# A recurrent attention loop with streamed weights: four places instead of five, one block more kept, 16 streamed

## The chip, the cores and the metric

The kernel runs on one core of one Trainium2 chip. The metric is the time of the whole program on the device in microseconds; lower is better. An execution under the profiler gives the span from the first to the last instruction, and a trace from which every view below is read.

## The reference

Two independent computations, put side by side along the last axis. Part A is a recurrent transformer layer: 2048 tokens in 64 segments of 32, each with 8 memory rows that are the first 8 output rows of the segment before. 32 heads of 128, model width 1024.

```python
mem = mem0
for s in range(n_seg):                                   # 64 segments
    xs = x[:, s * seg_len:(s + 1) * seg_len, :]
    h = jnp.concatenate([mem, xs], axis=1)               # 8 + 32 rows
    q = jnp.einsum('btd,dhe->bhte', h, Wq)               # Wq, Wk, Wv: [1024, 32, 128]
    k = jnp.einsum('btd,dhe->bhte', h, Wk)
    v = jnp.einsum('btd,dhe->bhte', h, Wv)
    scores = jnp.einsum('bhqe,bhke->bhqk', q, k) * scale
    scores = jnp.where(mask[None, None], scores, -1000000000.0)
    p = softmax(scores, axis=-1)
    o = jnp.einsum('bhqk,bhke->bhqe', p, v)
    o = jnp.einsum('bhte,hed->btd', o, Wo)               # Wo: [32, 128, 1024]
    mem = o[:, :M, :]
    outs.append(o[:, M:, :])
```

Part B is a long convolution: a kernel `K` of 2048 steps for each of 1024 channels is made from complex exponentials, and `u` is convolved with it by Fourier transforms.

## The kernel before

The program runs part B first (`part_b`), then part A (`part_a`). While part B runs, work of part A that doesn't depend on the recurrence is done beside it: projections of the last 8 rows of each segment, kept in DRAM (`PKd`), transposed inputs (`XTd`), and loads of weight blocks that will stay in SBUF.

**Weight blocks.** The four weights are cut into 64 blocks of 128 x 2048 bf16, 512 KB each. A key names a block: `("k", t, kc)` is the part of Wk for input rows 128 kc to 128 kc + 127 and the 16 heads of half t, likewise "q" and "v"; `("o", u)` holds heads 2u and 2u+1 of Wo. In every segment all 64 are needed once. Not all fit in SBUF, so there are three kinds:

- resident blocks (`RESIDENT`, line 171): loaded once, 34 of them during part B and the rest at their first use in segment 0;
- two blocks in PSUM (`KEPT`, line 28): `("k", 0, 7)` and `("o", 15)`, copied to pieces in SBUF by VectorE in each segment (`fetch`, line 278);
- streamed blocks (`STREAM`, `STREAM_O`, lines 25 and 26): 17 of them, fetched from a DRAM copy (`WD`) in every segment. They share `SLOTS` = 5 places in SBUF, tags w0 to w4, in turn.

**Order of a segment.** Lines 435 to 526 write it out by hand (`tc.manual_schedule()`; program order is the order on each engine): projections k0, q0, k1, q1, v0, v1 with `quads` (line 321; eight units of four matmuls, one for each block), transposes, scores and softmax of the two halves between them, then the output projection `oproj` over o0 to o15 (line 423), and at the end the result `ob`, whose first 8 rows go by two transposes (`tro`, line 523) into `hT`, the transposed input of the next segment. All projections of a segment wait for that: the loop is a chain from segment to segment.

**How a streamed block is loaded.** `unit` (line 235) is called by `quads` and `oproj` for each key. For a streamed one it does this:

```python
between.pop(key, lambda: None)()
t_ = wst.tile([128, 2048], BF16, name="wst", tag="w%d" % (loads[0] % SLOTS))
loads[0] += 1
nc.sync.dma_start(out=t_[:], in_=WD[key][:])
```

The load goes on SyncE's (SP's) queue. It must wait until TensorE has released the same place, that is until the streamed block `SLOTS` earlier has been used; SP is free to run that far ahead. SP's queue is in order: a transfer that waits holds up the ones behind it.

**Side transfers.** Three kinds of smaller transfers use the same queue, and `between` says ahead of which streamed block each is put. `load_pk` (line 292) fetches the projected last rows of this segment, 192 KB; its tile `pk` is also used as working space (`lb0a`, `pb1`), so it waits for the last reader in the segment before, `pv_l` at line 510. `stores` (line 309) writes the previous segment's `ob` to `OLd` and to the output, 64 KB each; it waits for the last copy into `ob` (line 526). `load_xt` (line 297) fetches the next segment's transposed input, 48 KB; its tile shares a place (tag F) with `lb0b`, and `put_xt` copies it into `hT`.

Of the kernel before, what the change touches and what calls it, by code (L numbers as in the profile page):

```python
# [21 lines left out]

STREAM = {("k", 0): (0, 5), ("q", 0): (1, 5), ("k", 1): (0, 3), ("q", 1): (0, 4), ("v", 0): (0, 4), ("v", 1): (0, 4)}
STREAM_O = (0, 4, 8, 11, 13)

KEPT = {("k", 0, 7): (("B", 0, 512), ("C", 512, 512), ("A", 1024, 512), ("F", 1536, 256), ("L", 1792, 256)),
        ("o", 15): (("B", 0, 512), ("C", 512, 512), ("E", 1024, 512), ("F", 1536, 256), ("L", 1792, 256))}
SLOTS = 5  # L30


def weight_blocks(Wq, Wk, Wv, Wo):
# [15 lines left out]
def streamed_keys():  # L49
    return [key for key in [(m, t, kc) for (m, t), kcs in STREAM.items() for kc in kcs] + [("o", u) for u in STREAM_O]]  # L50

# [136 lines left out]
def part_a(ctx, tc, x, mem0, src, WD, HE, seg_len, out_a, ahead, W_res, rest):  # L188
# [44 lines left out]
    between = {}  # L233

    def unit(key):
# [8 lines left out]
# [3 lines that stand above are left out]
# [45 lines left out]
    def load_pk(j):  # L292
        pk = pers.tile([128, 768], BF16, name="pk", tag="pk")
        nc.sync.dma_start(out=pk[:], in_=PKd[j])
        return pk

    def load_xt(j):
        xt = work.tile([128, KC, XM], BF16, name="xt", tag="F")
        nc.sync.dma_start(out=xt[:].rearrange("p k r -> p (k r)"), in_=XTd[j])
        return xt  # L300

    def put_xt(xt):
        nc.gpsimd.tensor_copy(out=hT[:, :, 0:XM], in_=xt[:])  # L303
# [5 lines left out]
    def stores(s, ob):  # L309
        nc.sync.dma_start(out=OLd[s // 8][:, 256 * (s % 8):256 * (s % 8) + 256], in_=ob[:, 1, :])  # L310
        rows = out_a[s * SL:s * SL + SL, :].rearrange("r (q d) -> q r d", q=4)
        if s + 1 < NS:

            nc.sync.dma_start(out=rows, in_=ob[:, 0, :])
        else:
            for q in range(4):
                nc.sync.dma_start(out=rows[q][0:XM], in_=ob[32 * q:32 * q + XM, 0, :])

    fetch(("k", 0, 7))
    for s in range(NS):  # L320
        def quads(m, t, kcs, a=None):
            if a is None:

                pool, tag = {("q", 0): (ps_sc, "sc"), ("q", 1): (ps_pv, "pv")}.get((m, t), (ps_acc, "acc"))
                a = pool.tile([128, 512], F32, name="acc", tag=tag)
            for kc in kcs:
                w = unit((m, t, kc))
                for g in range(4):
                    for o_, rhs in columns(w, 512 * g, 512):
                        nc.tensor.matmul(a[32 * g:32 * g + 32, o_:o_ + rhs.shape[1]], lhsT=hT[:, kc, :], rhs=rhs,  # L330
                                         start=(kc == 0), stop=(kc == KC - 1), tile_position=(0, 32 * g), skip_group_check=True)
            return a
# [90 lines left out]
        def oproj(po, us, oT):  # L423
            for u in us:
                w = unit(("o", u))
                for hh in range(2):
                    h = 2 * u + hh
                    for qt in range(4):
                        nc.tensor.matmul(po[32 * qt:32 * qt + 32, :], lhsT=oT[:, h % 4, (h % 16) // 4, :],  # L429
                                         rhs=columns(w, 1024 * hh + 256 * qt, 256)[0][1],  # L430
                                         start=False, stop=(h == 31), tile_position=(0, 32 * qt), skip_group_check=True)
# [2 lines left out]


        pks = []
        between["q", 0, 1] = lambda: pks.append(load_pk(s))
        if s:
            between["k", 1, 3] = lambda: stores(s - 1, ob)
        a = quads("k", 0, range(KC))  # L440
        k0 = evac(a, "A")
        a = quads("q", 0, range(KC))
# [66 lines left out]
        oproj(pp[:, 1, :], (7,), o0)  # L509
        pv_l(pl_, 1, V1, L1)  # L510
        if s + 1 < NS:
            between["o", 13] = lambda: put_xt(load_xt(s + 1))
        oproj(pp[:, 1, :], range(8, 14), o1)
        fetch(("o", 15))
        oproj(pp[:, 1, :], range(14, 16), o1)
        ob = work.tile([128, 2, 256], BF16, name="ob", tag="E")
# [677 lines left out]
def kernel(  # L1194
# [55 lines left out]
    with ExitStack() as ctx_a:  # L1250
        part_a(ctx_a, tc, A_x[0], A_mem0[0], src, WD, A_Wo.shape[0] * A_Wo.shape[1], seg_len, out_a, ahead, W_res, rest)
# [35 lines left out]
```

## Time and profile before

| | us |
|---|---|
| median of 3 runs | 2549.41 |
| lowest and highest run | 2538.42, 2555.1 |
| span of the profiled execution | 2562.5 |
| first matmul of the loop | 881.5 |
| end of the last turn from a segment to the next | 2468.6 |
| TensorE busy (matmuls) | 2055.3 (80%) |
| VectorE busy | 1498.0 (58%) |
| ScalarE busy | 1023.9 (40%) |
| GpSimd busy | 311.6 (12%) |

The span is all that the page tells of the profiled execution's own time; it is 13 us over the median of the runs, which were not profiled.

How to read the views: busy rows and DMA rows come in 40 slices of the span, each digit the busy share in tenths. A line of a wait says engine and source line, what it waited for, and then the total in us, the number of times and the longest. A line of the timeline says start, duration, engine, source line, operation, and in brackets the engine's idle time before it with what ended that. For SP, "SPq" lines are the issues of transfers: they begin when the transfer's waits are over, and end when SP is free for the next one; the data move later. L330 are the projections, L429 the output projection, L247 the loads of streamed blocks (tile `wst`), L294, L299, L310 and L314 the side transfers `pk`, `xt`, `OLd` and `out`.

Besides these views the prediction uses the landing events of transfers that the trace records: the time of the last update of a transfer's semaphore.

### The profile page before, as it was taken

The numbers are of one execution on the slowest core, as the hardware profiler recorded it, in microseconds if no ns is written. First come the engines' busy times: TensorE is split into PE (matmuls) and PEld (weight loads), VectorE is DVE, ScalarE is ACT, GpSimd is POOL, SyncE is SP. The second block draws the span as 40 slices with busy tenths as digits, with TensorE's granted clock in tenths as the row PEclk, the third lists the DMA queues.
The fourth block names the chain that finished last, engine by engine and source line by source line (L and its number), as shares of the span: only waits on it lengthen the run. The fifth ranks groups of instructions, "written<-read, shape, count | busy, mean of one in ns | idle before, by whom it ended". The sixth has DMA issues, their size and how long they took to land.

```text
span 2562.5 us, 76703 instructions
## 1 busy us (share of the span) xinstructions
PE 2055.3 (80%) x32856; PEld 1101.7 (43%) x32902; DVE 1498.0 (58%) x3224; ACT 1023.9 (40%) x1550; POOL 311.6 (12%) x601
## 2 busy tenths in 40 slices
PE   1588888857697778888888888888888888888879
PEld 1355555633242334444444444444444444444444
DVE  9687777879985245545454554545455454545450
ACT  6788788961121223323333332323333232333321
POOL 2133424442001100000000000000000000000020
PEclk6799999978898889999999999999999999999999
DMA  5665756543346999999999999999999999999992
GB/s 135 174 190 155 229 173 176 149 146 116 125 132 212 339 382 379 378 380 365 386 362 381 372 386 369 362 373 369 390 383 384 380 364 374 369 370 373 374 384 74
DMA packets 382387, 763.18 MB, mean 298 GB/s; under 512 B 118678, under 2 KB 210806, under 8 KB 379998
## 3 DMA queue, kind: packets, MB, share of 16 engines
q1 hardware_dynamic: 363006, 700.44, 76.1%
q0 software_dynamic: 14128, 39.99, 4.6%
q10 hardware_dynamic: 4912, 17.84, 2.0%
q8 instruction: 257, 4.21, 0.6%
q14 instruction: 84, 0.69, 0.1%
HBM read 703.35 MB, written 67.88 MB: 301 GB/s over the span
## 4 chain that ended last, share of the span: by engine, by line
DMA 33%; PE 28%; DVE 17%; ACT 9%; issue 8%; SPq 1%; POOL 0%; ACTq 0%; DVEq 0%; POOLq 0%
DMA wst<-WD_k 16%; PE acc L330 12%; DMA wst<-WD_o 10%; PE pp L429 3%; DMA wst<-WD_v 3%; PE pe L552 2%; ACT sn L1019 2%; PE pro L151 2%; PE tr L341 2%; ACT kM L994 1%; DVE piece L269 1%; PE ups L850 1%; ACT E L991 1%; PE pro L138 1%; ACT ev L336 1%
## 5 line engine op out<-in xcount | busy, mean ns | idle before, releaser
L330 PEld LDWEIGHTS <-hT 128*32 128x32 bf16 x12352 | 326.8, 97 | 474.1 <-issue 256.0
L330 PE MATMUL acc<-wst,hT 128*32 128x512 bf16 x3072 | 313.6, 393 | 163.3 <-DMA wst<-WD_k 67.4
L336 ACT CAST ev<-acc 128x512 bf16<-128x512 f32 x384 | 225.1, 586 | 414.4 <-PE acc L330 409.4
L429 PEld LDWEIGHTS <-oT 128*32 128x32 bf16 x8192 | 204.5, 97 | 116.6 <-issue 90.4
L269 DVE TENSOR_SCALAR piece<-keep 128x256 int32<-128x256 int32 (+1 forms) x640 | 191.4, 363 | 56.5 <-PE pp L429 31.1
L429 PE MATMUL pp<-W_o,oT 128*32 128x256 bf16 x5120 | 212.5, 277 | 6.8 <-DMA W_o<-in_A_Wo_dram 6.8
L330 PE MATMUL acc<-W_v,hT 128*32 128x512 bf16 x3072 | 211.1, 379 | 0.3 <-DMA W_v<-in_A_Wv_dram 0.3
L368 DVE TENSOR_REDUCE mx<-sc 128x8 f32<-128x320 f32 x128 | 62.4, 487 | 251.8 <-PE sc L361 251.6
L330 PE MATMUL acc<-W,hT 128*32 128x512 bf16 x2560 | 205.7, 392 | 0.0
L342 DVE COPY KT<-tr 128x512 bf16<-128x512 bf16 x64 | 27.2, 425 | 264.3 <-PE tr L341 264.3
L429 PE MATMUL pp<-wst,oT 128*32 128x256 bf16 x2560 | 129.2, 278 | 39.3 <-DMA wst<-WD_o 30.3
L342 ACT COPY QT<-tr 128x512 bf16<-128x512 bf16 x128 | 75.0, 586 | 192.6 <-PE tr L341 191.7
L1159 PE MATMUL yp<-Bt,mi 128*128 128x512 bf16 x379 | 115.5, 411 | 41.5 <-DMA mi<-MId 32.2
L416 ACT CAST oT<-pv 128x512 bf16<-128x512 f32 x128 | 75.1, 586 | 169.3 <-PE pv L402 166.9
L349 POOL COPY KT<-pk 128x128 bf16<-128x128 bf16 x128 | 37.6, 293 | 816.0 <-PE sc L361 454.4
L330 PE MATMUL acc<-W_q,hT 128*32 128x512 bf16 x1792 | 135.1, 383 | 0.0
L995 DVE SCALAR_TENSOR_TENSOR nr<-kM,ptt 128x656 f32<-128x656 f32 x128 | 104.9, 833 | 44.3 <-ACT kM L994 44.1
L151 PE MATMUL pro<-xTl,wsl 128*128 128x512 bf16 x493 | 116.6, 384 | 12.7 <-DVE kst L155 7.5
L370 ACT ACTIVATE sc<-sc 128x320 f32<-128x320 f32 x128 | 54.0, 422 | 154.8 <-DVE sc L369 148.0
L330 PE MATMUL acc<-W_k,hT 128*32 128x512 bf16 x1536 | 112.6, 401 | 0.0
L303 POOL COPY hT<-xt 128x192 bf16<-128x192 bf16 x64 | 22.2, 347 | 728.1 <-DMA xt<-XTd 442.0
L1075 PE MATMUL hps<-KT,MF 128*128 128x512 bf16 x374 | 93.3, 395 | 19.9 <-DVE x L1088 19.4
(288 smaller groups left out, 3766.7 us busy)
## 6 DMA issues: line engine op xcount, KB each, us to landing
wst<-WD_o SPq DMA_DIRECT2D x320, 512.0 KB
wst<-WD_k SPq DMA_DIRECT2D x256, 512.0 KB
wst<-WD_q SPq DMA_DIRECT2D x256, 512.0 KB
wst<-WD_v SPq DMA_DIRECT2D x256, 512.0 KB
Ud<-ux POOLq DMA_DIRECT2D x16, 1024.0 KB, 4.8
uq<-Ud SPq DMA_DIRECT2D x32, 512.0 KB
pk<-PKd SPq DMA_DIRECT2D x64, 192.0 KB
wsl<-in_A_Wk_dram SPq DMA_DIRECT2D x16, 512.0 KB
```

Source lines behind the costliest of these rows:

```text
L151: nc.tensor.matmul(a[:], lhsT=w[:, kc, 128 * j:128 * j + 128], rhs=xTl[:, kc, :, :].rearrange("p s k -> p (s k)"), start=(kc == 0), stop=( ...
L269: nc.vector.tensor_scalar(out=out.bitcast(I32), in0=in_.bitcast(I32), scalar1=0, scalar2=None, op0=ALU.bitwise_or)
L330: nc.tensor.matmul(a[32 * g:32 * g + 32, o_:o_ + rhs.shape[1]], lhsT=hT[:, kc, :], rhs=rhs, start=(kc == 0), stop=(kc == KC - 1), tile_pos ...
L336: nc.scalar.copy(out=q[:], in_=a[:])
L342: eng(out=dst, in_=p[:, i, :, :, :])
L368: nc.vector.tensor_reduce(out=mx[:], in_=sc, axis=AX.X, op=ALU.max)
L370: nc.scalar.activation(out=sc, in_=sc, func=ACT.Exp, scale=scale)
L416: nc.scalar.copy(out=o[:], in_=p[:].rearrange("p a (g q) -> p a g q", g=4))
L429: nc.tensor.matmul(po[32 * qt:32 * qt + 32, :], lhsT=oT[:, h % 4, (h % 16) // 4, :], rhs=columns(w, 1024 * hh + 256 * qt, 256)[0][1], star ...
L995: v.scalar_tensor_tensor(out=nrs[e // 4][:, e % 4].rearrange("p f t j -> p f (t j)"), in0=kM[:], scalar=MAGIC, in1=ptv, op0=ALU.subtract, ...
L1075: pe.matmul(ps[:], lhsT=MF[:, 4 * rr + mc, cs, 128 * kc:128 * kc + 128], rhs=rhs, start=(i == 0 and mc == 0), stop=(i == 1 and mc == 3))
L1159: pe.matmul(yp[:], lhsT=m_[:, cs, kc, :], rhs=Bt[:, kc, half, j, c_, :], start=(n == 0), stop=(n == 15))
```

## The change

The streamed blocks have four places instead of five. The fifth place's 512 KB hold one resident block more, so 16 blocks are streamed in each segment instead of 17, and which ones they are is chosen anew: k0: 0 and 6; q0: 4; k1: 1 and 6; q1: 0 and 6; v0: 2 and 6; v1: 0 and 4; o: 0, 6, 8, 11, 14. The three side transfers are put ahead of other blocks: `pk` ahead of q0:4, `stores` ahead of k1:1, `xt` ahead of o11. They stay on SP's queue. The order of the matmuls, transposes, softmax parts and copies in a segment stays as it is; only which units read a streamed place differs.

```diff
-STREAM = {("k", 0): (0, 5), ("q", 0): (1, 5), ("k", 1): (0, 3), ("q", 1): (0, 4), ("v", 0): (0, 4), ("v", 1): (0, 4)}
-STREAM_O = (0, 4, 8, 11, 13)
+STREAM = {("k", 0): (0, 6), ("q", 0): (4,), ("k", 1): (1, 6), ("q", 1): (0, 6), ("v", 0): (2, 6), ("v", 1): (0, 4)}
+STREAM_O = (0, 6, 8, 11, 14)
...
-SLOTS = 5
+SLOTS = 4
...
-        between["q", 0, 1] = lambda: pks.append(load_pk(s))
+        between["q", 0, 4] = lambda: pks.append(load_pk(s))
         if s:
-            between["k", 1, 3] = lambda: stores(s - 1, ob)
+            between["k", 1, 1] = lambda: stores(s - 1, ob)
...
-            between["o", 13] = lambda: put_xt(load_xt(s + 1))
+            between["o", 11] = lambda: put_xt(load_xt(s + 1))
```

## The prediction

> **What bounds the kernel now.** I read the page first. Its digit rows (40 slices of 64 us) show two halves: part B up to slice 13, then the recurrent loop, where the DMA engines stand at 9 in every slice and PE at 8.
>
> ```profile
> PE   1588888857697778888888888888888888888879
> DMA  5665756543346999999999999999999999999992
> GB/s 135 174 190 155 229 173 176 149 146 116 125 132 212 339 382 379 378 380 365 386 362 381 372 386 369 362 373 369 390 383 384 380 364 374 369 370 373 374 384 74
> ```
>
> Neither row alone says who waits. So I asked for windows over the loop (columns: length, busy of PE, PEld, DVE, ACT, POOL, clock, DMA share, GB/s) and for PE's waits between 930 and 2468 us.
>
> ```profile
> 923.00:1300.00 377.00, 320.09 (x6447) 167.87 (x6451) 196.50 (x546) 116.50 (x226) 14.30 (x46) 0.98 1.00 376
> 1700.00:2100.00 400.00, 337.27 (x6866) 176.83 (x6866) 208.34 (x577) 124.66 (x242) 14.98 (x49) 1.00 1.00 380
> PE acc L330 <- DMA wst<-WD_k: 61.4, 71, 2.1
> PE acc L330 <- DMA wst<-WD_q: 49.1, 102, 2.3
> PE tro L523 <- DVE ob L518: 27.8, 62, 0.5
> PE pp L429 <- DMA wst<-WD_o: 22.7, 42, 1.3
> PE acc L330 <- DMA wst<-WD_v: 3.5, 7, 1.0
> ```
>
> DMA share is 1.00, and PE loses 61.4 + 49.1 + 22.7 + 3.5 = 137 us to streamed blocks. The `tro` transposes mark the segments: 62 of them from 923 to 2469 us, mean 24.93 us, 9.35 MB each. PE's own timeline at one segment boundary, with its idle time in brackets:
>
> ```profile
> 1543.51 0.40 PE L330 MATMUL acc<-wst,hT 128*32 128x512 bf16 x4 [0.33 <-PE tro L523]
> 1546.31 0.40 PE L330 MATMUL acc<-wst,hT 128*32 128x512 bf16 x4 [0.67 <-DMA wst<-WD_q]
> 1547.57 0.40 PE L330 MATMUL acc<-wst,hT 128*32 128x512 bf16 x4 [0.22 <-DMA wst<-WD_q]
> 1549.07 0.40 PE L330 MATMUL acc<-wst,hT 128*32 128x512 bf16 x4 [0.33 <-DMA wst<-WD_k]
> 1551.17 0.40 PE L330 MATMUL acc<-wst,hT 128*32 128x512 bf16 x4 [1.27 <-DMA wst<-WD_k]
> ```
>
> PE starts each block 0.05 us after it lands. From 1546.31 to 1547.57 is 1.26 us: two blocks, back to back. The landing events of the trace give the same everywhere: 1.27 us is the usual distance of two 512 KB blocks, 413 GB/s. About 18% of the blocks come some 0.76 us later than that, at no fixed place. I call these hiccups, and have no cause for them. The queue of SP in the same stretch:
>
> ```profile
> 1535.39 0.32 SPq L299 DMA_DIRECT2D xt<-XTd  x1
> 1535.80 1.41 SPq L247 DMA_DIRECT2D wst<-WD_o  x1
> 1537.30 0.86 SPq L247 DMA_DIRECT2D wst<-WD_k  x2
> 1539.95 0.32 SPq L294 DMA_DIRECT2D pk<-PKd  x1
> 1540.51 0.97 SPq L247 DMA_DIRECT2D wst<-WD_q  x2
> 1541.76 0.32 SPq L247 DMA_DIRECT2D wst<-WD_k  x1
> 1543.19 0.32 SPq L310 DMA_DIRECT2D OLd<-ob  x1
> 1543.57 0.56 SPq L314 DMA_DIRECT2D out_dram<-ob  x1
> 1544.23 0.92 SPq L247 DMA_DIRECT2D wst<-WD_k  x1
> ```
>
> The block issued at 1544.23 is the one PE takes at 1551.17, 6.9 us later. That is queueing: it stands behind four or five transfers of 1.27 us. SP stalls 1.8 us before `pk` (1538.16 to 1539.95), but the transfers issued before are still under way, so nothing goes empty. So the loop is bound by bytes.
>
> **What the Trainium skill says.** "DMA: Bandwidth & Descriptors", section "Queues, rings and completion order": descriptors of one issuing engine's queue are consumed in ring order. The trace agrees for loads: blocks land in the order of issue. Same page, "Measured": 425 GB/s is the best of its table (16 MB), so a block at 413 GB/s can't get much faster. Same page, "Anatomy of one DMA": a fixed cost of about 2 us beside the moving of data (its fit is for the GpSimd path). The trace bounds it for SP: the shortest issue-to-landing of a block in the loop is 3.78 us, its predecessor landing 1.26 us before it; so the fixed part is at most 2.5 us. The very first block, with little ahead of it, went from issue at 878.24 to PE at 881.51: 3.3 us. "Perfetto Trace Analysis", section "DMA Instruction — HWDGE (DVE, Sync)": semaphores are waited for at the sequencer, before descriptors are made; so what stands behind a waiting transfer on SP waits too. The `pk` stall above shows it.
>
> **The change, part by part.**
>
> *One block fewer per segment.* Sum of landing distances in a mean segment before: 17 blocks, the two stores (about 0.5), `pk` (0.71) and `xt` (0.18) make 24.95, which is the segment. Sixteen blocks apart from the one behind the stores have a mean of 1.39 us (1.27 and its share of hiccups). One block less saves 1.39 us, or 1.27 if the hiccups go by time instead of by block.
>
> *What is late next: PE's own chain.* From the timeline without its DMA waits: a unit of 4 matmuls takes 0.2153 us; transposes 0.46 a group; scores, values, output projection and the turn of the segment as seen. The streamed units then start, counted from `k0:0`, at: after the change k0 at 0 and 1.29; q0 2.58; k1 4.12 and 5.65; q1 6.65 and 7.94; v0 9.26 and 10.58; v1 11.94 and 13.47; o 14.71, 16.03, 18.28, 18.93 and 19.59; next segment at 21.57. Clock dips (13 of 3 us at half clock in the loop, 1.5 us each) add 0.3. PE needs 21.9, the stream 24.95 - 1.39 = 23.56. The stream stays the bound.
>
> *Four places instead of five.* A block can be issued when the one four earlier is released: 0.40 us after its unit starts, and 0.04 to SP. It needs 3.78 us to land and 0.05 to PE. So two units four places apart must be 4.27 us apart, or PE waits even with an idle stream. In the new spread these distances are 5.54, 4.58, 5.22, 6.10, 5.65, 5.36, 5.36, 5.14, 4.93, 5.29, 5.53, 5.45, 5.45, 6.34, 5.46, 4.88: all enough. (The old spread with four places would fail twice, k1:0 with 3.90 and k1:3 with 3.48.) Four places in steady flow give 4 x 1.27 = 5.08 us for a cycle of 4.27: enough to keep the stream full while PE takes blocks as they land. Cost: none in the mean, some in the hiccups (bounds 0 and 0.3 us).
>
> *Side transfers.* `xt` moves ahead of o11's load instead of o13's; both of these wait for the release of v1:4 and `xt` for `lb0b`, free by then: same instant, nothing. `pk` moves ahead of q0:4's load; the load before it (k0:6) waits for o8, which PE runs after the last reader of `pk`: its 1.8 us stall goes. It hid behind queued transfers, so it is worth nothing by itself (bounds 0 and 0.1). The stores move from the sixth place to the fourth. They wait for `ob`, ready 0.32 us before `k0:0`. Behind them on SP is the load of k1:1, whose place was free since o14 (19.99, that is 1.58 us before `k0:0`): the wait is new. With the stores' own issue it goes out at +0.72 us, as the load behind the stores does now (1544.23 against 1543.51). It lands at +0.72 + 3.78 = 4.50; PE wants it at 4.12. So the stream runs dry there for about 0.37 us in every segment. With 3.3 us instead of 3.78 it lands at 4.02, in time: bounds 0 and 0.4. I take 0.37, since in the loop nothing under 3.78 is seen. `ob` shares its place with `QT`: the copy to QT0 at about 5.2 waits for the stores to land; with three transfers ahead of them instead of five they land sooner than now. Nothing.
>
> *Resident blocks and first segment.* One more block is kept, and loaded once, in the first segment. That segment moves 11 + 17 weight blocks now and 12 + 16 then: the same. The prologue's copies to DRAM are one fewer, in part B, where the row shows 116 to 229 GB/s: nothing. Last stage: the same six loads.
>
> *Sum.* -1.39 + 0.37 = -1.02 us in each of 63 segments: -64 us. On the profiled execution 2562.5 - 64 = 2498. The median of the runs, 2549.41, is 13 us under that span; the loop is the same in both, so 2549.4 - 64 = **2485 us**.
>
> **The rivals.**
> 1. *Late loads don't bite, or PE drinks faster:* fixed part as with the first block. 1.39 us in 63 segments are 88 us: 2462. For it: the 3.3 us. Against: PE at 21.9 comes within 1.7 us of the stream, so some hiccups will be paid twice.
> 2. *Thin cover:* with one place less, hiccups and the store wait add up, each late load lasting. If the loss per segment is 1.1 instead of 0.37, 0.29 x 63 = 18 us remain: 2531, within 1%. For it: distances 4.58 and 4.88 are only 0.3 and 0.6 above 4.27, less than a hiccup.
> 3. *Slower: four places can't fill the pipe.* Landings in the loop take mostly 5.4 to 7 us from issue. I read that as queueing. If it is latency of loaded memory, a cycle is latency + 0.49 us, and four places pass one block each quarter of it. The point of decision: 24.93 less 0.9 for the side transfers is 24.0; over 16 blocks 1.50; times 4, 6.0 us a cycle, a latency of 5.5. At 6.0 us: 6.49/4 x 16 + 0.9 = 26.9 us, 2.0 x 63 = +124: 2673. Against it: 3.78 us with a full queue, and blocks 1.27 us apart whatever the latency.
> 4. The change not taking effect can be left aside: all three `between` places are streamed keys, so each side transfer is issued, and the program has one load less in each segment.
>
> **How the numbers follow.** My forecast's case has 0.60, rival 1 0.18, rival 2 0.12, rival 3 0.10. A measurement of this kernel tells about 1% (25 us) from no change. Faster by over 1% are the forecast and rival 1, 0.78; rival 2 counts as same, 0.12; slower 0.10. The forecast's own bounds: 1.27 to 1.39 saved, 0 to 0.7 lost at the stores and in hiccups: 0.57 to 1.39 us, 2462 to 2514. For 8 in 10 the range goes a little below rival 1 and up to rival 2: 2452 to 2532.
>
> **What would show it right or wrong.** Right: segment mean near 23.9 us at 9.35 - 0.52 = 8.82 MB, so 369 GB/s; PE's waits for `wst` from 137 to about 100 us; SP's wait before L294 gone, its wait before L310 longer; blocks still 1.27 us apart; a wait of PE at the fourth block (k1:1) in most segments. Wrong: the rate falls below 355 GB/s, with landings over 1.5 us apart at many places (rival 3), or waits for `wst` above 137 us (rival 2).

## The result, and the profile after

The changed kernel takes 2652.95 us (median of 4 runs, 2650.69 to 2658.39), beside 2546.61 us for the kernel before (median of 4; three of them are the runs of the table above): 1.043 times, 95% interval 1.039 to 1.047. It is slower by 106 us. The forecast was 2485 us, a gain of 64.

The page of the kernel after, slices of 66 us. The loop begins at slice 13:

```profile
PE   1588788675978688887887888888888878888878
DMA  5665854743349999999999999899999999999992
GB/s 138 172 192 164 251 167 132 195 121 118 114 143 336 331 322 331 331 339 319 321 340 326 342 331 340 316 341 333 327 338 334 351 336 335 344 339 333 340 344 74
```

The bytes per segment fell as the change says: 8.82 MB in the mean of 62 segments, 9.35 before. But the rate fell more, from 375 to 334 GB/s, and the segment went from 24.93 to 26.49 us. The digit 9 in the DMA row hides it: a digit is a tenth, and 0.94 and 1.00 are both 9. The windows tell more (same columns as in the prediction, DMA share and GB/s last), and so do PE's waits between 930 and 2560 us:

```profile
930.00:1700.00 770.00, 629.23 (x12305) 323.69 (x12305) 375.63 (x1040) 222.81 (x434) 27.09 (x87) 0.95 0.94 331
1700.00:2550.00 850.00, 699.96 (x13797) 362.96 (x13795) 424.54 (x1170) 250.26 (x486) 29.89 (x96) 0.96 0.95 336
PE pp L429 <- DMA wst<-WD_o: 102.8, 142, 2.7
PE acc L330 <- DMA wst<-WD_v: 57.0, 81, 2.0
PE acc L330 <- DMA wst<-WD_k: 46.1, 50, 2.2
PE acc L330 <- DMA wst<-WD_q: 15.4, 34, 1.1
```

DMA share is 0.94 to 0.95 instead of 1.00: the engines now stand still for part of the time. That is about half of the 11% that the rate lost; the other half is in packets that take longer (last section). PE's waits for blocks are 221 us (102.8 + 57.0 + 46.1 + 15.4), 137 before, and they have moved: to the blocks of the output projection and of v, which cost 26 us before. SP's wait for `ob` ahead of the stores, before (930 to 2468 us) and after (930 to 2560 us):

```profile
SPq L310 <- ACT ob L526: 60.1, 61, 1.2
SPq L310 <- ACT ob L526: 146.2, 62, 4.4
```

One turn of a segment in the kernel after, SP's queue and PE at its streamed blocks (other lines left out):

```profile
1527.04 0.38 SPq L247 DMA_DIRECT2D wst<-WD_q  x1
1529.08 0.32 SPq L310 DMA_DIRECT2D OLd<-ob  x1
1529.49 0.55 SPq L314 DMA_DIRECT2D out_dram<-ob  x1
1530.14 0.90 SPq L247 DMA_DIRECT2D wst<-WD_k  x2
1529.40 0.40 PE L330 MATMUL acc<-wst,hT 128*32 128x512 bf16 x4 [0.33 <-PE tro L523]
1530.69 0.40 PE L330 MATMUL acc<-wst,hT 128*32 128x512 bf16 x4
1532.89 0.40 PE L330 MATMUL acc<-wst,hT 128*32 128x512 bf16 x4 [0.71 <-DMA wst<-WD_q]
1536.51 0.40 PE L330 MATMUL acc<-wst,hT 128*32 128x512 bf16 x4 [1.92 <-DMA wst<-WD_k]
```

SP stalls 1.7 us before the stores (1527.42 to 1529.08). The block issued behind them at 1530.14 is the one PE takes at 1536.51, 6.4 us later and 1.92 us late. In this segment it was worse than the mean: over all segments the block behind the stores lands 4.80 us after its issue. The prediction gave it 3.78.

**What the landings show.** I call *lead* the time by which a block's issue comes before the landing of the block ahead of it. With enough lead a block usually lands 1.27 us after that one. From the landing events, blocks that directly follow a block:

| lead, us | before: number, mean distance us | after: number, mean distance us |
|---|---|---|
| under 3.5 | 20, 2.06 | 198, 1.85 |
| 3.5 to 4.0 | 56, 1.59 | 172, 1.67 |
| 4.0 to 4.5 | 139, 1.46 | 201, 1.40 |
| 4.5 to 5.0 | 276, 1.35 | 130, 1.34 |
| over 5.0 | 363, 1.32 | 92, 1.29 |

Both kernels lie on one curve, which is flat only from 4.5 us up. The prediction took a lead of 2.5 us for enough. Before, three quarters of the blocks have over 4.5 us; after, 222 of 793. The signs that the prediction named for its rival 3 are there: a rate under 355 GB/s, and landings 1.55 us apart in the mean.

### The profile page after: what moved, and what is told of

The parts are those of the page before. It is cut to its first block, busy times and chain, and to the rows that moved or that the text cites. A ratio compares the mean times of both kernels' runs of the same rounds, so it can differ in the third digit from the quotient of the medians.

```text
span 2652.8 us, 76630 instructions
## 1 busy us (share of the span) xinstructions
PE 2091.5 (79%) x32902; PEld 1111.2 (42%) x32902; DVE 1500.2 (57%) x3224; ACT 1022.9 (39%) x1550; POOL 311.7 (12%) x601
## 4 chain that ended last, share of the span: by engine, by line
DMA 44%; PE 28%; DVE 13%; ACT 7%; issue 3%; POOL 0%; SPq 0%; ACTq 0%; DVEq 0%; POOLq 0%
DMA wst<-WD_o 16%; PE acc L330 14%; DMA wst<-WD_v 13%; DMA wst<-WD_k 8%; DMA wst<-WD_q 4%; PE pp L429 3%; PE pe L552 2%; ACT sn L1019 2%; PE pro L151 2%; PE yp L1159 2%; DVE m L1109 1%; DVE m L1108 1%; DVE m L1107 1%; ACT kM L994 1%; DVE x L1088 1%
## 5 line engine op out<-in xcount | busy, mean ns | idle before, releaser
L330 PEld LDWEIGHTS <-hT 128*32 128x32 bf16 x12352 | 336.6, 100 | 473.9 <-issue 256.3
L330 PE MATMUL acc<-wst,hT 128*32 128x512 bf16 x2816 | 295.4, 404 | 156.8 <-DMA wst<-WD_v 62.4
L330 PE MATMUL acc<-W_v,hT 128*32 128x512 bf16 x3072 | 238.7, 386 | 1.5 <-DMA W_v<-in_A_Wv_dram 1.5
L330 PE MATMUL acc<-W,hT 128*32 128x512 bf16 x2560 | 212.9, 449 | 0.0
L429 PE MATMUL pp<-W_o,oT 128*32 128x256 bf16 x5120 | 190.3, 276 | 7.5 <-DMA W_o<-in_A_Wo_dram 7.5
L330 PE MATMUL acc<-W_q,hT 128*32 128x512 bf16 x2048 | 147.3, 381 | 0.0
L330 PE MATMUL acc<-W_k,hT 128*32 128x512 bf16 x1536 | 132.2, 391 | 0.0
L519 ACT CAST ob<-pp 128x128 bf16<-128x128 f32 x64 | 17.0, 265 | 281.3 <-DVE ob L518 273.1
L518 DVE CAST ob<-pp 128x128 bf16<-128x128 f32 x64 | 18.7, 291 | 168.9 <-PE pp L429 168.9
## 6 DMA issues: line engine op xcount, KB each, us to landing
pk<-PKd SPq DMA_DIRECT2D x64, 192.0 KB
```

## The experiments

Three theories stood at the start: P (four places put too little in flight), W (the stores' new wait on SP's queue), and S (the new places of the streamed blocks in PE's order). Ratios are to the kernel before on the same chip.

### 16 streamed blocks, 5 places

```diff
-SLOTS = 4
+SLOTS = 5
+ALIAS = {("q", 0, 7): ("q", 0, 6)}
...
     def unit(key):
+        key = ALIAS.get(key, key)
```

> The changed kernel with the fifth place back: 16 streamed blocks, 5 places. To make room, block q0:7 is not kept; its unit reads the block q0:6 instead (that part of q is left out of the computation), the matmuls and all transfers are the same in number. Theory P (places: with four, too little is in flight to cover stalls of single DMA engines): the loop goes to its bytes again, 24.9 - 1.39 = 23.5 us a segment, about 2460 us in all. Theory W (the stores' new wait on SP's queue): that wait stays, so at most a third of the 106 us comes back, 2610 or more. Theory S (the new places of the streamed blocks in the order of the segment are the bad part): stays over 2600.

2546.71 us, ratio 1.000 (0.999 to 1.002). All 106 us come back, so P holds in the main and S falls; but none of the expected gain of 64 us appears. P alone is not all. SP's waits (930 to 2460 us) say what is left; in this kernel L312 are the stores, L301 `xt`:

```profile
SPq L312 <- ACT ob L528: 192.0, 61, 5.4
SPq L301 <- PE pv L404: 139.1, 61, 3.3
```

The stores stand before the fourth block of the segment, and with five places SP gets there a block earlier. It then waits 192.0 / 61 = 3.1 us for `ob`, while two further places have come free behind it.

### 17 streamed blocks, 4 places

```diff
-SLOTS = 5
+SLOTS = 4
```

> The kernel before with SLOTS = 4 and nothing else: 17 streamed blocks in the old places, side transfers where they were. Theory P: slower than the changed kernel's 2653, since 17 blocks go through four places: 26.5/16 x 17 = 28.1 us a segment, about 2750 us. Theory W: about 2550 to 2600, since the stores' wait is where it was. Theory S: about 2550 to 2600.

2721.9 us, ratio 1.070 (1.067 to 1.074). Taking the fifth place alone from the kernel before costs 173 us. W and S are absent here, so neither is needed for a loss of this size. The prediction's own rule has two late blocks in the old spread, by 0.37 and 0.79 us (its 3.90 and 3.48 against 4.27): 73 us, less than half of it. A segment is 27.57 us. With 0.9 us off for `pk` and `xt` that is (27.57 - 0.9) / 17 = 1.57 us a block, against (24.93 - 0.9) / 17 = 1.41 with five places.

### The changed kernel with the stores later

```diff
-            between["k", 1, 1] = lambda: stores(s - 1, ob)
+            between["k", 1, 6] = lambda: stores(s - 1, ob)
```

> The changed kernel with the stores put ahead of k1:6 instead of k1:1, so that no load of a block waits behind ob at the turn of a segment. Theory W: most of the 106 us come back, below 2590. Theory P: only what the wait itself costs, 0.4 us (the prediction's figure) to 1.5 us in each of 63 segments, 2560 to 2630; the low end only if the store wait is the larger part. Theory S: as P's high end, 2630.

2631.98 us, ratio 1.034 (1.029 to 1.039): 21 us back, a third of a microsecond in each of 63 segments: a little less than the least that P gave the wait. A segment is 26.20 us, so a block is (26.20 - 0.9) / 16 = 1.58 us: as in the old places with 17 blocks. Here the pace goes with the number of places, not with the spread.

### 17 streamed blocks, 6 places

`SLOTS = 6` in the kernel before, with the same alias.

> The kernel before with a sixth place: 17 streamed blocks, SLOTS = 6; block q0:7 is not kept, its unit reads block q0:6 (that part of q is left out of the computation). It shows how much cover five places lacked. Theory P in its strong form (each place more covers more stalls): 24.9 to about 24.3 us a segment, 2510. If the stream is at its engines' own pace with five places already (the DMA share of the window is 1.00): no change, 2540 to 2550.

2547.36 us, ratio 0.999 (0.998 to 1.001). A sixth place gives nothing by the medians: with 17 blocks and five places the engines are at their pace, as the prediction read from the DMA share.

### 16 streamed blocks, 5 places, stores at the sixth block

The first experiment (`SLOTS = 5`, q0:7 reads q0:6), with the stores in another place:

```diff
-            between["k", 1, 1] = lambda: stores(s - 1, ob)
+            between["q", 1, 0] = lambda: stores(s - 1, ob)
```

> As the run with 16 streamed blocks and 5 places (q0:7 not kept, its unit reads q0:6), with the stores moved back to the sixth place, ahead of q1:0, where the kernel before has them. Theory PW (both count: four places give too short a lead, and the stores' new wait on SP takes the lead away where it stands): the stream keeps its lead everywhere, and time follows bytes at last: 24.93 - 1.39 = 23.5 us a segment, 2460 us. If the stores' place means little: 2547 as with them at the fourth block, and then bytes are not the bound that I took them for, but PE's chain.

2482.65 us, ratio 0.976 (0.970 to 0.981). Here is the forecast's number, 2485, in a kernel that has the fifth place and the stores ahead of the sixth block, as before. Windows and PE's waits from 930 to 2400 us (L431 the output projection, L332 the others):

```profile
930.00:2400.00 1470.00, 1296.38 (x26557) 692.38 (x26559) 808.36 (x2243) 481.21 (x936) 62.40 (x194) 0.98 1.00 374
PE pp L431 <- DMA wst<-WD_o: 51.4, 80, 2.1
PE acc L332 <- DMA wst<-WD_q: 15.7, 32, 1.7
PE acc L332 <- DMA wst<-WD_v: 7.7, 15, 1.0
```

The share is 1.00 and the rate 374 GB/s again, with 8.82 MB a segment: here time follows bytes while the lead holds.

### 16 streamed blocks, 6 places, stores at the seventh block

`SLOTS = 6`, stores ahead of q1:6, and a second alias (q0:5 reads q0:3).

> 16 streamed blocks with 6 places, stores ahead of q1:6 (the seventh block); q0:7 and q0:5 are not kept, their units read q0:6 and q0:3. It is the most lead that 16 blocks get here. Theory PW: 2440 to 2460, within 20 us of the run with 5 places and late stores. If PE's chain is the bound at some 24.5 us: 2540.

2501.2 us, ratio 0.982 (0.978 to 0.986): slower than with five. A new wait took over, at the top of PE's list; below it what ScalarE waits for at that copy:

```profile
PE sc L359 <- ACT QT L344: 62.0, 58, 1.7
ACT QT L344 <- DMA OLd<-ob: 102.2, 40, 3.3
```

The copy to `QT` can't start until the stores have read `ob`, which has the same place in SBUF; behind more blocks they land too late.

### The kernel before with the stores one block earlier

```diff
-            between["k", 1, 3] = lambda: stores(s - 1, ob)
+            between["k", 1, 0] = lambda: stores(s - 1, ob)
```

> The kernel before, 17 streamed blocks and 5 places, with the stores one block earlier, ahead of k1:0 instead of k1:3: the load of k1:0, whose place is free since o13, then waits on SP behind ob as k1:1's does in the changed kernel. Nothing else differs. Theory PW: one load a segment is late, 0.5 to 1.4 us in 63 segments: 2580 to 2640. If a store wait is covered by five places: 2550.

2584.68 us, ratio 1.015 (1.010 to 1.020). W by itself, 38 us, without any change of places or bytes. One position in SP's in-order queue was worth 0.6 us in each segment.

### Half places

The changed kernel with stores ahead of k1:6, `SLOTS = 8`, and each block loaded as two halves (the cut of the code leaves out that the two PSUM blocks are loaded in halves too):

```diff
-        t_ = wst.tile([128, 2048], BF16, name="wst", tag="w%d" % (loads[0] % SLOTS))
-        loads[0] += 1
-        nc.sync.dma_start(out=t_[:], in_=WD[key][:])
-        return t_
+        parts = []
+        for n in range(2):
+            t_ = wst.tile([128, 1024], BF16, name="wst", tag="w%d" % (loads[0] % SLOTS))
+            loads[0] += 1
+            nc.sync.dma_start(out=t_[:], in_=WD[key][:, 1024 * n:1024 * n + 1024])
+            parts.append((1024 * n, 1024, t_))
+        return parts
```

> The changed kernel with stores ahead of k1:6 and each of the four places cut in two: a streamed block comes as two transfers of 256 KB (128 rows of 2 KB), into 8 half places, and each half is given back when its two of the unit's four matmuls are done. Same SBUF, same bytes. Theory PW: 7 halves in flight behind the one awaited give a lead of 7 x 0.635 - 0.45 = 4.0 us instead of 3 x 1.27 - 0.45 = 3.4, which by the table of lead and landing is worth 0.1 to 0.2 us a block: about 2632 - 16 x 0.15 x 63 = 2480 to 2530. Against it: rows of 2 KB may move slower, and SP issues twice as often; if that weighs more, over 2632.

2653.31 us, ratio 1.042 (1.037 to 1.047): worse than whole places with late stores (2632), and a miss. Halves with enough lead land 0.67 us apart, 1.34 for a block instead of 1.27. Why the longer lead on paper gains nothing in the loop was not settled; with the stream by itself it does gain, see next.

### The stream by itself

All of the computation is left out but the loads and four matmuls for each; the settings follow each other in one program.

```python
for name, places, cut, engs in STAGES:        # ("n4", 4, 1, ("sync",)) and so on
    for i in range(80):
        ...                                   # the load(s) of block i, into place i % places
        use(parts)                            # four matmuls
```

> The stream by itself: all of both parts is left out (the output holds copied inputs). 80 loads of 512 KB blocks from their DRAM copies for each of eight settings, one after the other, TensorE taking each block with four matmuls as soon as it lands: 6, 5, 4, 3 and 2 places on SP's queue; 4 places cut into 8 halves; 4 and 5 places with loads issued by SP and ACT in turn. Read: the mean time from block to block. The prediction's rule (a block needs 3.78 us from issue, a place comes back 0.49 us after landing) says 1.27 us with 6, 5 and 4 places, 1.42 with 3, 2.14 with 2. Theory L (the start of a transfer takes 2.5 to 4.5 us and differs from engine to engine, so a block needs 4.5 us or more of lead): about 1.30 with 6, 1.37 with 5, 1.57 with 4, over 1.9 with 3, over 2.5 with 2. Theory S (the uneven order in which the segment takes its blocks makes the loss): 1.27 to 1.32 with 4 places here. Halves: by L 1.45 to 1.6. Two queues: no difference to one, if what counts is bytes in flight.

| setting | us from block to block | the prediction's rule |
|---|---|---|
| 6 places | 1.28 | 1.27 |
| 5 places | 1.31 | 1.27 |
| 4 places | 1.49 | 1.27 |
| 3 places | 1.79 | 1.42 |
| 2 places | 2.46 | 2.14 |
| 4 places in 8 halves | 1.37 | |
| 4 places, SP and ACT in turn | 1.51 | |
| 5 places, SP and ACT in turn | 1.36 | |

(First matmul to first matmul, without the first 8 of 80, in one execution.) The windows of 5, 4, 3 and 2 places (length, busy of PE, PEld, DVE and POOL, clock, DMA share, GB/s):

```profile
181.00:272.00 91.00, 42.84 (x280) 7.68 (x276) 0.00 (x0) 0.00 (x0) 1.00 1.01 402
291.00:395.00 104.00, 42.71 (x280) 7.72 (x280) 0.00 (x0) 0.00 (x0) 1.00 0.97 350
401.00:541.00 140.00, 48.22 (x312) 8.66 (x312) 0.00 (x0) 0.00 (x0) 1.00 0.86 292
546.00:738.00 192.00, 48.23 (x316) 8.67 (x312) 0.00 (x0) 0.00 (x0) 1.00 0.69 213
```

Nothing else runs, the clock is at 1.00 throughout and PE takes each block at once, yet four places pass 350 GB/s and five 402. This settles the disputed step: 0.18 us a block between five and four, without order (S) or stores (W). The two settings with two queues, which come last, repeat it: 1.51 and 1.36. A block's four matmuls take 0.62 us here and 0.40 in the loop, so a place comes back some 0.2 us later than the prediction's rule has it. With that the rule would by estimate be 1.50 us with three places and 2.25 with two, and still 1.27 with four. With two places, issue to landing is 4.20 us in the mean and 3.20 at the least. The prediction had a lowest value, where a mean and its spread were needed. A second queue gave nothing.

### 15 streamed blocks, 4 places, stores later

v0:6 is not streamed but reads v0:5.

> The changed kernel with stores ahead of k1:6 and one streamed block fewer: v0:6 is not streamed, its unit reads the kept block v0:5 (that part of v is left out). 15 streamed blocks, 4 places. If each block costs the pace of four places (1.49 us in the stream by itself, 1.58 as (26.2 - 0.9)/16 in the loop with 16 blocks and late stores): 2632 less 63 x 1.5 to 1.6 = 2531 to 2537, no better than the kernel before with 17 blocks and five places, give or take. If the loop were near PE's own chain by then, less would be gained: 2560.

2581.01 us, ratio 1.016 (1.010 to 1.022), 51 us under 16 blocks where 95 to 101 were expected: a miss. Most of what is left, 81 of PE's 134 us of waits for blocks, stands at one spot (930 to 2400 us):

```profile
PE pp L431 <- DMA wst<-WD_o: 80.8, 97, 2.2
```

The block taken away stood among v's; the o blocks come as close together as before. So read, a short lead is a local matter, and a mean pace times blocks is no good forecast for taking one away; this was not tested further. Still, two blocks less than before don't pay for the fifth place.

### 16 streamed blocks, 6 places, stores at the sixth block

The six places again, with stores ahead of q1:0.

> 16 streamed blocks and 6 places again (q0:7 and q0:5 not kept, their units read q0:6 and q0:3), with the stores ahead of q1:0 instead of q1:6. With q1:6 the copy to QT0 waited for the stores to land (PE 1.0 us a segment at L359), since QT shares its place with ob. If that was what made six places slower than five, it is gone here: 2470 to 2485, the same as five places with stores at q1:0 within 10 us, since the stream by itself gains only 1.31 to 1.28 us a block. If not: 2500.

2465.79 us, ratio 0.970 (0.965 to 0.975). PE's wait at L359 has gone from 62.0 us to 1.5:

```profile
PE sc L359 <- ACT QT L344: 1.5, 5, 0.6
```

So it was the shared place of `ob` and `QT` that had made six places slower. By the medians six are then 17 us better than five, but the two ratios' intervals overlap, so a gain over five places is not shown.

No version with all its blocks was faster than the kernel before. The faster runs above buy their room by not keeping one or two blocks, so part of q is left out of what they compute: they show causes, and are no kernels to use.

## Why the prediction was wrong

The medians of four kernels split the 106 us. The first step holds several edits, and its kernel reads q0:6 for q0:7. The second takes the fifth place and keeps q0:7 again; its stores move up with the places, so that in both kernels the block behind them takes the place of k0:0, which comes free only after `ob`. The last step is one edit:

| step | median us | change | the prediction |
|---|---|---|---|
| before (beside the run in the next row) | 2546.4 | | |
| one block less, new spread, `pk` and `xt` moved; five places, stores sixth | 2482.7 | -64 | -1.39 a segment, -88, less cover in hiccups |
| four places instead of five, stores fifth | 2632.0 | +149 | 0, at most 0.3 us a segment (+19) |
| stores at the fourth block | 2653.0 | +21 | +0.37 us a segment, +23 |

- *The bound* was read rightly: bytes. With the lead kept, one block less saved 64 us, 1.0 us a segment (1.27 to 1.39 expected); the profiled executions, 24.93 and 23.63 us a segment, say 1.3.
- *Four places instead of five* is the step that failed: put at 0 to 0.3 us a segment, it took 149 us, 2.4 us a segment. It compared distances of 4.58 us and more with a need of 4.27, built on the shortest issue-to-landing of some 850 blocks, 3.78 us, and called the fixed part "at most 2.5 us". Only five of those blocks took under 4 us. The lowest of many samples bounds the lowest, not the mean: in the stream alone a block takes 4.20 us with two places, so by estimate 4.20 - 1.27 = 2.9 us beside the moving of data, and it spreads. "The Trainium skill", "DMA: Bandwidth & Descriptors", section "Anatomy of one DMA", gives about 2 us for the GpSimd path; here, from SP, the measurement is higher and decides. And 5.08 us a cycle against a need with that spread is no slack: at the full pace four places would leave a lead of 3 x 1.27 - 0.45 = 3.4 us by estimate, five 4.6, on a curve that is flat from 4.5. So with four the pace falls until lead and distance agree: 4.1 and 1.55 us in the mean of the loop after.
- *The hiccups*, which I left without a cause, were in good part this: of the blocks before with a lead of 3.5 to 4.0 us, 45% come over 0.2 us late, with 4.0 to 4.5, 24%, with over 5 us, 6%. Of all such late blocks 74 of 127 had a lead under 4.5. The lead table could have been made from the trace of before.
- *The stores' wait* was right in mechanism. That 21 us came so near to the 23 is in part luck: the block behind the stores landed after 4.80 us and not 3.78, so it was 1.0 us later than reckoned, and PE's waits for k blocks, mostly this one, were 0.74 us a segment where 0.37 had been put (46.1 us over 62 segments). That its size depends on the places was missed: 64 us with five places and 16 blocks (2546.7 less 2482.7), 38 with the old spread.
- *`pk`, `xt`, first segment* were not tried one by one; the -64 against -88 leaves 24 us for them, the new spread and the hiccups together.
- *Rival 3* named the right mechanism and a time of 2673 us for it. It was given 0.10, on the argument that blocks land 1.27 us apart "whatever the latency"; but that was seen with five places, where the lead hides the latency. Neither reading was whole: with four places issue to landing fell from 6.26 to 5.62 us in the mean, so part of it was queueing.
- *The clock* is a rival that no run held fixed in the loop. It stood at half speed for 44 us of the 62 segments before (13 dips) and for 137 us after (36 dips), and PE was busy for 21.73 us a segment instead of 21.07. In the segments without any dip, 18 to 48 of each profile, the four kernels of the table take 24.62, 23.21, 25.22 and 25.99 us: steps of -1.41, +2.01 and +0.77. So most of the loss is there at full clock. The rest goes with the dips; whether the waiting brings more of them was not tested.

## What to carry to other kernels

Price the loss of a buffer by the distribution of issue-to-landing, not by its lowest value: group the landings by lead, find where the curve turns flat, and see what lead is left with one place less. Before trading buffers for bytes, measure the stream by itself with each number of places; here one run of it gave the sign. In an in-order queue, put a transfer that waits for the end of a step behind all loads whose places are free earlier, and look at who shares its tile.

## What was not expected of the hardware

Five places of 512 KB pass 402 GB/s and four 350. The mean of 4.20 us from issue to landing asks by estimate for no more than 4.20 x 413 GB/s = 1.7 MB in flight; four places are 2.1 MB, less the block in use, and still lose 13%. In the packet records of the loop the usual 4 KB packet takes 159 ns in both kernels; the mean is 171 before and 182 after, and the slowest hundredth 502 and 776 ns or more. The stream by itself shows it without the loop: a packet takes 164 ns in the mean with five places, 180 with four and 208 with two, and the slowest hundredth 172, 809 and 870 or more. So in these records single packets take longer when less is in flight. A block lands with its slowest part: of the 16 updates that tell of its landing, with two places, the first comes 2.8 us after issue, the middle ones 3.1 and the last 4.2. What holds the late packets was not found.
